# A decode attention block: key loads in runs of 16 KB, on half of the partitions each

## The chip, the core and the metric

The kernel runs on one core of a Trainium2 chip. Its time is the device time of one execution in microseconds (us). The core has five engines that run beside each other: TensorE (PE in the profile; PEld is its weight loads), VectorE (DVE), ScalarE (ACT), GpSimd (POOL) and SyncE (SP), which here issues the large transfers. Transfers from HBM into SBUF are moved by 16 DMA engines. SBUF and PSUM have 128 partitions.

## What is computed

Eight sequences (B = 8) take one decode step. The input is normalized; one branch is attention with 32 query heads and 8 key/value heads over the last W = 1024 of 4096 cached keys, the other a gated FFN whose result gates the attention's.

```python
W = min(4096, max(256, Sk // 4))                       # 1024
xn = _layernorm(x, axis=-1)
q = (xn @ wq) in 32 heads of 128
k, v = the last W rows of k_cache, v_cache, each of 8 heads used by 4 query heads
p = _softmax(q . k * Dh ** -0.5)
s = (p . v) @ wo
g = _silu((_gelu(xn @ w_gate) * (xn @ w_up)) @ w_down)
return x + s * g
```

All inputs are bf16. Keys and values of the window are 2 MB each for a head over all eight sequences (16.8 MB of keys, 16.8 MB of values); wq and wo are 4.2 MB each, the three FFN weights 1.8 MB each. That is 47.45 MB that go through the core once.

## The kernel before

**Tiling.** A *set* is four of the eight sequences for one key/value head (G = 4). There are NS = 16 sets, two for each head (NB = 2; set y of a head holds the sequences 2g + y). The keys of a set lie over 128 partitions: partition 4p + g holds 32 successive keys (8 KB) of sequence g, p = 0 to 31 (KP = 32, NCH = 32). Keys are taken as pairs, and a pair's 256 bf16 values are seen as 128 fp32 values, so that one fp32 transpose on TensorE turns 128 pairs at once.

**Loads.** `load_pair` (L104 to L116) brings both sets of a head into one tile of the pool `big` (nine buffers of 16 KB per partition) with one transfer of 2 MB (L109), or in two of 1 MB, one for each set and each over all partitions (L115; the first head of keys and the last of values). The runs in HBM are 8 KB. wq, the FFN weights, keys, values and wo all use tiles of this pool in turn; wo comes in five pieces (L623 to L627, issued at L130). All are issued by SP, in program order, each waiting until the buffer that it overwrites has been used and until the eighth transfer before it has landed (eight completion semaphores are used in turn). `fetch` (L554) issues them in the order K0, K1, K2, w_down, V0, K3, V1, K4, ... V4, K7, V5, V6, V7.

**Order of the work.** The order on each engine is the program's order, written out by hand in one loop (L571 to L604) over steps t. For a set s the steps are:

- `transpose_quarter(s, 0..3)` (L430) at t = 2s and 2s + 1: four fp32 transposes each into one PSUM tile, copied to `kT` in SBUF by DVE (L444) and ACT (L446) in turn. `kT` holds one set.
- `scores(s)` (L450) at t = 2s + 2, `maxima(s)` (L471) at 2s + 3, `exponentials(s)` (L485) and `turn(s)` (L496, a 32x32 block transpose of the probabilities) at 2s + 4.
- `value_half(s, 0..1)` (L504) at t = 2s + 9 and 2s + 10 (LV = 9), and `gather(h)` (L520), which sums a head's parts and divides by the sum of the exponentials, at t = 4h + 13.
- The FFN's second matmul (`down`, L398) and its gate at t = 8 to 10.

After the loop `project` (L609) multiplies by wo, DVE gates and adds x (L633, L634), and two small transfers write the output.

The score of a key must stand where the value of the same key stands: `own`, `turn` and `value_half` all take keys in the order (p, g) in which the values lie on the partitions.

Of the kernel before, what the change touches and what calls it, by code (L numbers as in the profile page):

```python
# [11 lines left out]
BF16 = mybir.dt.bfloat16  # L12
FP32 = mybir.dt.float32
# [4 lines left out]
def kernel(  # L18
# [13 lines left out]
    nc = tc.nc  # L32

    B, Sq, D = A_x.shape
    Hkv, Sk, Dh = A_k_cache.shape[1], A_k_cache.shape[2], A_k_cache.shape[3]
    Hq = A_wq.shape[1] // Dh
    rep = Hq // Hkv
    W = min(4096, max(256, Sk // 4))
    win0 = Sk - W
# [4 lines left out]
    P = nc.NUM_PARTITIONS  # L44
# [3 lines left out]

    G = 4
    NB = B // G
    NS = Hkv * NB
    KP = P // G
    NCH = W // KP
    NC = G * rep
    SET = NCH * Dh
    QT = 4
    CP = NCH // 2
    QP = CP // QT  # L60
# [7 lines left out]


    lead = ctx.enter_context(tc.tile_pool(name="lead", bufs=1))  # L70
    big = ctx.enter_context(tc.tile_pool(name="big", bufs=9))
    kT_pool = ctx.enter_context(tc.tile_pool(name="kT_pool", bufs=2))
    p_pool = ctx.enter_context(tc.tile_pool(name="p_pool", bufs=2))
    consts = ctx.enter_context(tc.tile_pool(name="consts", bufs=1))
# [3 lines left out]
    ps_kT = ctx.enter_context(tc.tile_pool(name="ps_kT", bufs=4, space=PSUM))  # L78
# [15 lines left out]
    def load_rows(w, r0, n, per, name):  # L94

        t = big.tile([P, 2 * SET], BF16, name="big")
        cols = w.shape[1]
        nc.sync.dma_start(  # L98
            out=t[:, 0 : n * cols],
            in_=w.rearrange("(p k) n -> p k n", p=P)[:, r0 : r0 + n, :],  # L100
        )
        return t[:, 0 : n * cols].rearrange("p (k n) -> p k n", k=n)

    def load_pair(cache, h, parts=1):  # L104

        t = big.tile([P, NB, SET], BF16, name="big")
        src = cache[:, h, win0:Sk, :]
        if parts == 1:
            nc.sync.dma_start(  # L109
                out=t, in_=src.rearrange("b (p c) d -> p b (c d)", p=KP)  # L110
            )
        else:
            src = src.rearrange("(g y) (p c) d -> y p g (c d)", y=NB, p=KP)
            for y in range(NB):
                nc.sync.dma_start(out=t[:, y, :], in_=src[y])  # L115
        return [t[:, y, :].rearrange("p (c d) -> p c d", c=NCH) for y in range(NB)]  # L116

    HB = 2 * SET // (rep * D)
    wo_tiles = {}
# [23 lines left out]
    for k0, cuts in ((0, (1, 1)), (2, (2,))):  # L143
        t = big.tile([P, 2, Hq * Dh], BF16, name="big")
        i = 0
        for n in cuts:
            nc.sync.dma_start(  # L147
                out=t[:, i : i + n, :],
                in_=A_wq.rearrange("(p k) n -> p k n", p=P)[:, k0 + i : k0 + i + n, :],
# [277 lines left out]

    K, V, kT, sc, P_, pT, blk = {}, {}, {}, {}, {}, {}, {}

    def transpose_quarter(s, i):  # L430
        ps = ps_kT.tile([P, QP, P], FP32, name="kT_ps")
        for c in range(QP):
            nc.tensor.transpose(  # L433
                ps[:, c, :],
                K[s][:, 2 * (i * QP + c) : 2 * (i * QP + c) + 2, :]
                .rearrange("p c d -> p (c d)").bitcast(FP32),
                identf,
            )
        if i == 0:
            kT[s] = kT_pool.tile([P, CP, P, 2], BF16, name="kT")  # L440
        out = kT[s][:, i * QP : (i + 1) * QP].rearrange("p c k e -> p (c k e)")
        in_ = ps.rearrange("p c k -> p (c k)").bitcast(BF16)
        if i % 2 == 0:
            nc.vector.tensor_copy(out=out, in_=in_)  # L444
        else:
            nc.scalar.activation(out=out, in_=in_, func=ACT.Copy)  # L446
# [2 lines left out]

    def scores(s):  # L450
        ps = ps_sc.tile([P, CP, 32], FP32, name="sc")
        t = kT.pop(s)
        for e in range(2):
            for R in range(NR):
                nc.tensor.matmul(  # L455
                    ps[32 * R : 32 * R + 32],
                    qT[:, e, s].rearrange("p c b j -> p (c b j)"),
                    t[:, :, 32 * R : 32 * R + 32, e],
                    start=(e == 0), stop=(e == 1), skip_group_check=True,
                )  # L460
        sc[s] = small.tile([P, CP * 32], FP32, name="sc_sb", bufs=2)
        top[s] = small.tile([P, 1], FP32, name="top")
        nc.vector.tensor_tensor_reduce(  # L463
            out=sc[s], in0=ps.rearrange("p c k -> p (c k)"),
            in1=own.rearrange("p c b g -> p (c b g)"),
            op0=ALU.add, op1=ALU.max, scale=1.0, scalar=NEG, accum_out=top[s],
        )
# [3 lines left out]
    def maxima(s):  # L471

        ps = m_top
        nc.tensor.matmul(  # L474
            ps, top.pop(s).to_broadcast([P, P]), identf, start=True, stop=True
        )
        scr = small.tile([P, P], FP32, name="scr", bufs=1)
        bias = small.tile([P, 1], FP32, name="bias")
        nc.vector.tensor_tensor_reduce(  # L479
            out=scr, in0=ps, in1=same.rearrange("p x n -> p (x n)"),  # L480
            op0=ALU.add, op1=ALU.min, scale=-scale, scalar=-NEG, accum_out=bias,
        )
        biases[s] = bias

    def exponentials(s):  # L485
        blk[s] = small.tile([P, 2, Dh + 1], FP32, name="blk", bufs=6)
        P_[s] = p_pool.tile([P, CP * 32], BF16, name="p")
        nc.scalar.activation(  # L488
            out=P_[s], in_=sc.pop(s), func=ACT.Exp, scale=scale, bias=biases.pop(s),
            accum_out=blk[s][:, 0, Dh : Dh + 1],  # L490
        )
        nc.gpsimd.tensor_copy(  # L492
            out=blk[s][:, 1, Dh : Dh + 1], in_=blk[s][:, 0, Dh : Dh + 1]
        )

    def turn(s):  # L496
        pT[s] = p_pool.tile([P, CP, 32], BF16, name="pT", bufs=5)
        nc.vector.transpose(  # L498
            out=pT[s].rearrange("p c k -> p (c k)"), in_=P_.pop(s)
        )  # L500
# [19 lines left out]
    def gather(h):  # L520

        ps = m_out
        for b in range(NB):
            t = blk.pop(h * NB + b)
            for c in range(2):
                nc.tensor.matmul(  # L526
                    ps, sums[:, c, b].rearrange("p j b f -> p (j b f)"), t[:, c, :],
                    start=(b == 0 and c == 0), stop=(b == NB - 1 and c == 1),
                )
        rec = small.tile([P, 1], FP32, name="rec")  # L530
        nc.vector.reciprocal(out=rec, in_=ps[:, Dh : Dh + 1])
        o = small.tile([P, rep, Dh // rep], BF16, name="o")
        nc.vector.tensor_scalar(
            out=o, in0=ps[:, 0:Dh].rearrange("p (i r) -> p r i", r=rep),
            scalar1=rec, scalar2=None, op0=ALU.mult,
        )


        out = oL[:, NS2 * h : NS2 * h + PB, 0:OL]
        out = out.rearrange("p f (r y) -> p r y f", y=OW)  # L540
        nc.vector.transpose(  # L541
            out=out[:, :, 0 : B * NS2 : NS2, :], in_=o.rearrange("p r i -> p (r i)")
        )
# [10 lines left out]
    def fetch(kind, h):  # L554
        while True:
            k, i = pending.pop(0)
            if k == "D":
                down_tiles.append(load_rows(B_w_down, 0, NFC, NFC, "wd"))
            else:
                sets = load_pair(  # L560
                    A_k_cache if k == "K" else A_v_cache, i,
                    2 if (k, i) in (("K", 0), ("V", Hkv - 1)) else 1,
                )
                for y in range(NB):
                    (K if k == "K" else V)[NB * i + y] = sets[y]
            if (k, i) == (kind, h):
                return


    LV = 4 * AHEAD - 3  # L570
    for t in range(2 * NS + LV + 3):  # L571
        s, i = divmod(t, 2)
        if i == 0 and 0 <= s - 2 < NS:
            exponentials(s - 2)
        if s < NS:
            if i == 0 and s % NB == 0:
                fetch("K", s // NB)
            transpose_quarter(s, 2 * i)
        if i == 1 and s >= 6 and s % 2 == 0:
            gather((s - 6) // 2)  # L580
        if s < NS:
            transpose_quarter(s, 2 * i + 1)
        for _ in range(2):
            if hidden_steps:
                hidden_steps.pop(0)()
        if i == 0 and 0 <= s - 2 < NS:
            turn(s - 2)
        if i == 0 and 0 <= s - 1 < NS:
            scores(s - 1)
        if i == 1 and 0 <= s - 1 < NS:  # L590
            maxima(s - 1)
        if t == LV - 1:
            fetch("D", 0)
            down(0)
        if t == LV:
            down(1)
        if t == LV + 1:
            fold()
            gate()
        s3, i3 = divmod(t - LV, 2)  # L600
        if 0 <= s3 < NS:
            if i3 == 0 and s3 % NB == 0:
                fetch("V", s3 // NB)
            value_half(s3, i3)  # L604
# [15 lines left out]
                    skip_group_check=True,  # L620
                )

    pieces = [(0, 0, rep, 4), (4, 0, rep, 2), (6, 0, rep, 1)]  # L623

    pieces += [(Hkv - 1, 0, rep - 1, 1), (Hkv - 1, rep - 1, 1, 1)]
    for h0, r0, nr, nh in pieces:
# [43 lines left out]
```

## Time and profile before

| | |
|---|---|
| Runs | 120.46, 120.54, 120.80 us (median 120.54) |
| Profiled execution | 120.65 us, span 118.8 us from the first to the last instruction |
| Granted TensorE clock | 0.979 on average |
| Bytes read from HBM | 47.46 MB, 400 GB/s over the span |
| Key loads | 7 of 2048 KB, 2 of 1024 KB; median 34.1 and 21.3 us from issue to landing |
| Transposes of keys (L433) | 256, 38.5 us of PE |
| Copies to `kT` | DVE (L444) 32 x 688 ns, ACT (L446) 32 x 1021 ns |

The profile's page gives the busy time of each engine, then the span in 40 equal slices (busy tenths of each engine and of the DMA engines, with GB/s), the DMA queues, the chain of work that ended last, followed back from the last instruction, and the costliest groups of instructions. "SPq" in the chain is SP issuing a transfer. The trace also has a record of each packet that a DMA engine moves, with its size and duration: a packet is one run of bytes into one partition.

### The profile page before, as it was taken

Reading aid. Unit: us, or ns where it says so; the run is one execution under the profiler, and the core shown is the slowest. Engines: PE = TensorE matmul, PEld = TensorE weight load, DVE = VectorE, ACT = ScalarE, POOL = GpSimd, SP = SyncE. Lnnn points to the kernel's source line nnn. Section 1 sums busy time; section 2 is a strip of 40 time slices with the busy share of each in tenths; the row PEclk is TensorE's granted clock in tenths of the full one; section 3 lists DMA queues with packets and bytes.
Section 4 is the critical chain, followed back from the end, with each engine's and each line's share of the span. In section 5 each row is a group of like instructions: output and inputs, shape, how many; then the busy total and the mean of one; then the engine's idle time right before and its main releaser. Section 6 shows DMA issues by size and latency. Waiting matters only on the chain.

```text
span 118.8 us, 2387 instructions
## 1 busy us (share of the span) xinstructions
PE 84.4 (71%) x974; PEld 59.2 (50%) x974; DVE 66.3 (56%) x171; ACT 56.2 (47%) x94; POOL 7.5 (6%) x28
## 2 busy tenths in 40 slices
PE   0070629599492999699969869787795988676670
PEld 0020216198262677377746557555573755555660
DVE  1310131837799766678848658585773965834301
ACT  0500030229808667575854884676565577132000
POOL 7700000000000000000000000000000000000000
PEclk9999999999999599999999999999999999999997
DMA  3999999999999999999999999999999999999940
GB/s 94 430 450 436 406 444 405 433 430 419 422 462 412 412 428 433 417 428 428 425 425 428 422 436 422 422 433 425 425 425 425 428 428 430 408 421 421 420 170 3
DMA packets 6569, 47.60 MB, mean 401 GB/s; under 512 B 536, under 2 KB 672, under 8 KB 1696
## 3 DMA queue, kind: packets, MB, share of 16 engines
q1 hardware_dynamic: 6512, 47.45, 95.2%
q8 instruction: 7, 0.11, 0.3%
q10 hardware_dynamic: 48, 0.01, 0.1%
q14 instruction: 2, 0.02, 0.0%
HBM read 47.46 MB, written 0.01 MB: 400 GB/s over the span
## 4 chain that ended last, share of the span: by engine, by line
DMA 86%; SPq 6%; PE 4%; issue 0%; DVE 0%
DMA big<-in_A_k_cache_dram 72%; DMA big<-in_A_wo_dram 14%; SPq L130 4%; PE kT_ps L433 3%; SPq L147 1%; SPq L98 1%; PE s L615 1%; PE sc L455 0%; DVE tmp L633 0%; DVE out_sb L634 0%; PE o_ps L509 0%
## 5 line engine op out<-in xcount | busy, mean ns | idle before, releaser
L446 ACT ACTIVATE kT<-kT_ps 128x1024 bf16<-128x1024 bf16 x32 | 32.5, 1021 | 23.6 <-PE kT_ps L433 23.5
L433 PE MATMUL kT_ps<-identf,big 128*128 128x128 f32 x256 | 38.5, 296 | 5.2 <-DMA big<-in_A_k_cache_dram 5.1
L433 PEld LDWEIGHTS kT_ps<-identf,big 128*128 128x128 f32 x256 | 30.9, 151 | 13.2 <-DMA big<-in_A_k_cache_dram 7.0
L444 DVE COPY kT<-kT_ps 128x1024 bf16<-128x1024 bf16 x32 | 22.0, 688 | 15.2 <-PE kT_ps L433 15.0
L488 ACT ACTIVATE p<-sc_sb,bias 128x512 bf16<-128x512 f32 x16 | 11.5, 717 | 7.0 <-DVE bias L479 6.5
L509 PE MATMUL o_ps<-big,pT 128*32 128x256 bf16 x256 | 12.3, 274 | 3.0 <-ACT blk L516 1.6
L498 DVE STREAM_TRANSPOSE pT<-p 128x512 bf16<-128x512 bf16 x16 | 11.3, 704 | 2.8 <-ACT p L488 2.8
L474 PE MATMUL m_ps<-identf,top 128*128 128x128 f32 x32 | 7.3, 309 | 6.0 <-DVE top L463 4.3
L463 DVE CUSTOM_DVE_ANT_0 sc_sb<-sc,own 128x512 f32<-128x512 f32 x16 | 10.5, 656 | 0.5 <-PE sc L455 0.5
L455 PE MATMUL sc<-kT,zeros 128*32 128x512 bf16 x128 | 10.3, 398 | 0.5 <-ACT kT L446 0.5
L509 PEld LDWEIGHTS <-pT 128*32 128x32 bf16 x256 | 5.8, 94 | 8.0 <-DMA big<-in_A_v_cache_dram 2.2
L526 PE MATMUL m_ps<-blk,sums 128*128 128x129 f32 x64 | 9.3, 286 | 0.0
L492 POOL COPY blk<-blk 128x1 f32<-128x1 f32 x16 | 2.9, 184 | 96.5 <-ACT p L488 92.2
L474 PEld LDWEIGHTS m_ps<-identf,top 128*128 128x128 f32 x32 | 4.8, 187 | 8.1 <-DVE top L463 5.0
L526 PEld LDWEIGHTS m_ps<-blk,sums 128*128 128x128 f32 x64 | 8.1, 191 | 0.9 <-issue 0.2
L516 ACT ACTIVATE blk<-o_ps 128x256 f32<-128x256 f32 x16 | 6.1, 381 | 3.0 <-PE o_ps L509 3.0
L541 DVE STREAM_TRANSPOSE oL<-o 128x128 bf16<-128x128 bf16 x8 | 6.0, 748 | 0.3
L310 PE MATMUL sc<-big,zeros 128*32 128x512 bf16 x16 | 2.5, 611 | 4.6 <-DMA big<-in_A_wq_dram 4.2
L615 PE MATMUL s<-big,oL 128*32 128x128 bf16 x128 | 4.3, 219 | 1.9 <-DMA big<-in_A_wo_dram 1.9
L317 DVE CAST q_row<-sc 128x512 bf16<-128x512 f32 x2 | 1.3, 686 | 7.8 <-PE sc L310 7.8
L615 PEld LDWEIGHTS <-oL 128*32 128x32 bf16 x128 | 3.8, 96 | 2.5 <-issue 2.3
L479 DVE CUSTOM_DVE_ANT_0 scr<-m_ps,same 128x128 f32<-128x128 f32 x16 | 4.9, 304 | 0.1
(70 smaller groups left out, 51.5 us busy)
## 6 DMA issues: line engine op xcount, KB each, us to landing
big<-in_A_k_cache_dram SPq DMA_DIRECT2D x7, 2048.0 KB, 34.1
big<-in_A_v_cache_dram SPq DMA_DIRECT2D x7, 2048.0 KB, 33.1
big<-in_A_wq_dram SPq DMA_DIRECT2D x2, 1024.0 KB, 5.8
big<-in_A_wq_dram SPq DMA_DIRECT2D x1, 2048.0 KB, 11.2
big<-in_A_k_cache_dram SPq DMA_DIRECT2D x2, 1024.0 KB, 21.3
big<-in_A_v_cache_dram SPq DMA_DIRECT2D x2, 1024.0 KB, 30.3
big<-in_A_wo_dram SPq DMA_DIRECT2D x1, 2048.0 KB, 30.9
big<-in_B_w_gate_dram SPq DMA_DIRECT2D x1, 1792.0 KB, 15.0
```

What stands on the lines that cost most here:

```text
L433: nc.tensor.transpose(ps[:, c, :], K[s][:, 2 * (i * QP + c) : 2 * (i * QP + c) + 2, :] .rearrange("p c d -> p (c d)").bitcast(FP32), identf,)
L444: nc.vector.tensor_copy(out=out, in_=in_)
L446: nc.scalar.activation(out=out, in_=in_, func=ACT.Copy)
L455: nc.tensor.matmul(ps[32 * R : 32 * R + 32], qT[:, e, s].rearrange("p c b j -> p (c b j)"), t[:, :, 32 * R : 32 * R + 32, e], start=(e == ...
L463: nc.vector.tensor_tensor_reduce(out=sc[s], in0=ps.rearrange("p c k -> p (c k)"), in1=own.rearrange("p c b g -> p (c b g)"), op0=ALU.add, ...
L474: nc.tensor.matmul(ps, top.pop(s).to_broadcast([P, P]), identf, start=True, stop=True)
L488: nc.scalar.activation(out=P_[s], in_=sc.pop(s), func=ACT.Exp, scale=scale, bias=biases.pop(s), accum_out=blk[s][:, 0, Dh : Dh + 1],)
L498: nc.vector.transpose(out=pT[s].rearrange("p c k -> p (c k)"), in_=P_.pop(s))
L509: nc.tensor.matmul(o_ps[s][32 * q : 32 * q + 32].rearrange("p c d -> p (c d)"), pT[s][:, c, :], V[s][:, 2 * c : 2 * c + 2, :].rearrange("p ...
L516: nc.scalar.activation(out=blk[s][:, :, 0:Dh], in_=o_ps.pop(s), func=ACT.Copy)
L526: nc.tensor.matmul(ps, sums[:, c, b].rearrange("p j b f -> p (j b f)"), t[:, c, :], start=(b == 0 and c == 0), stop=(b == NB - 1 and c == 1),)
L615: nc.tensor.matmul(s_ps[32 * g : 32 * g + 32, :], t[:, a : a + OW], w[:, q * 128 : (q + 1) * 128], start=(h == 0 and r == 0 and s == 0), s ...
```

## The change

- Keys get a loader of their own, `load_keys`. For each set y of a head one transfer brings its keys to 64 partitions (64y to 64y + 63): partition 64y + 4p + g holds 64 successive keys (16 KB) of sequence 2g + y, p = 0 to 15. A head takes two transfers of 1 MB, all heads 16. Values are loaded as before.
- One transpose now turns 64 pairs of each of the two sets. `transpose_part(h, i)`, i = 0 to 7, replaces the quarters of two sets; each has four transposes and one copy, so that the counts stay the same. A partition of keys holds the keys of two partitions of values (u = 0, 1), so each transpose writes its columns into PSUM with a gap: runs of four (g), then four left out for the other u, at places (y, c, p, u, g). With that the order (p, u, g) is that of the values. `kT` now holds a head (two buffers as before, each twice as large).
- To make room the pool `big` has eight buffers instead of nine.
- `scores`, `maxima`, `exponentials` and `turn` of set s are two steps later (t = 2s + 4, 2s + 5, 2s + 6, 2s + 6). `value_half`, `gather` and the FFN stay at their steps.
- wo is loaded in six pieces: its first four heads come in two transfers instead of one.

```diff
-    big = ctx.enter_context(tc.tile_pool(name="big", bufs=9))
+    big = ctx.enter_context(tc.tile_pool(name="big", bufs=8))
...
+    def load_keys(h):
+        t = big.tile([P, NB * SET], BF16, name="big")
+        src = A_k_cache[:, h, win0:Sk, :].rearrange(
+            "(g y) (p c) d -> y p g (c d)", y=NB, p=KP // NB
+        )
+        for y in range(NB):
+            nc.sync.dma_start(out=t[y * P // NB : (y + 1) * P // NB, :], in_=src[y])
+        return t.rearrange("p (c d) -> p c d", d=Dh)
...
-    def transpose_quarter(s, i):
-        ps = ps_kT.tile([P, QP, P], FP32, name="kT_ps")
-        for c in range(QP):
-            nc.tensor.transpose(
-                ps[:, c, :],
-                K[s][:, 2 * (i * QP + c) : 2 * (i * QP + c) + 2, :]
-                .rearrange("p c d -> p (c d)").bitcast(FP32),
-                identf,
-            )
+    def transpose_part(h, i):
+        ps = ps_kT.tile([P, NB, QP // NB, KP // NB, NB, G], FP32, name="kT_ps")
+        for c in range(QP // NB):
+            for u in range(NB):
+                k0 = u * NCH + 2 * (i * QP // NB + c)
+                nc.tensor.transpose(
+                    ps[:, :, c, :, u, :],
+                    K[h][:, k0 : k0 + 2, :].rearrange("p c d -> p (c d)").bitcast(FP32),
+                    identf.rearrange("p (y b g) -> p y b g", y=NB, g=G),
+                )
         if i == 0:
-            kT[s] = kT_pool.tile([P, CP, P, 2], BF16, name="kT")
+            kT[h] = kT_pool.tile([P, NB, CP, P, 2], BF16, name="kT")
...
     def scores(s):
-        t = kT.pop(s)
+        t = kT[s // NB][:, s % NB]
...
     for t in range(2 * NS + LV + 3):
-        s, i = divmod(t, 2)
-        if i == 0 and 0 <= s - 2 < NS:
-            exponentials(s - 2)
+        h, i = divmod(t, 4)
+        s = due(t, 6)
+        if s is not None:
+            exponentials(s)
...
-    pieces = [(0, 0, rep, 4), (4, 0, rep, 2), (6, 0, rep, 1)]
+    pieces = [(h, 0, rep, 2) for h in range(0, Hkv - 2, 2)] + [(Hkv - 2, 0, rep, 1)]
```

(`due(t, d)` gives s where t = 2s + d.)

More of the change, by code (lines that the diff above doesn't have):

```diff
@@ L428 @@
     K, V, kT, sc, P_, pT, blk = {}, {}, {}, {}, {}, {}, {}
-    def transpose_quarter(s, i):
-        ps = ps_kT.tile([P, QP, P], FP32, name="kT_ps")
-        for c in range(QP):
-            nc.tensor.transpose(
-                ps[:, c, :],
-                K[s][:, 2 * (i * QP + c) : 2 * (i * QP + c) + 2, :]
-                .rearrange("p c d -> p (c d)").bitcast(FP32),
-                identf,
-            )
+    def transpose_part(h, i):
[8 more added lines that the diff above has]
+                )
         if i == 0:
-            kT[s] = kT_pool.tile([P, CP, P, 2], BF16, name="kT")
-        out = kT[s][:, i * QP : (i + 1) * QP].rearrange("p c k e -> p (c k e)")
-        in_ = ps.rearrange("p c k -> p (c k)").bitcast(BF16)
+            kT[h] = kT_pool.tile([P, NB, CP, P, 2], BF16, name="kT")
+        n = QP // NB
+        out = kT[h][:, :, i * n : (i + 1) * n].rearrange("p y c k e -> p y (c k e)")
+        in_ = ps.rearrange("p y c b u g -> p y (c b u g)").bitcast(BF16)
         if i % 2 == 0:
@@ L558, in fetch @@
                 down_tiles.append(load_rows(B_w_down, 0, NFC, NFC, "wd"))
-            else:
[L560 to L563, printed above, removed]
+            elif k == "K":
+                K[i] = load_keys(i)
+            else:
+                sets = load_pair(A_v_cache, i, 2 if i == Hkv - 1 else 1)
                 for y in range(NB):
-                    (K if k == "K" else V)[NB * i + y] = sets[y]
+                    V[NB * i + y] = sets[y]
             if (k, i) == (kind, h):
@@ L570, with due @@
     LV = 4 * AHEAD - 3
+    def due(t, d):
+        s, r = divmod(t - d, 2)
+        return s if r == 0 and 0 <= s < NS else None
     for t in range(2 * NS + LV + 3):
-        s, i = divmod(t, 2)
-        if i == 0 and 0 <= s - 2 < NS:
-            exponentials(s - 2)
[L575 to L582, printed above, removed]
+        h, i = divmod(t, 4)
+        s = due(t, 6)
+        if s is not None:
+            exponentials(s)
+        if h < Hkv:
+            if i == 0:
+                fetch("K", h)
+            transpose_part(h, 2 * i)
+        if i == 1 and h >= 3:
+            gather(h - 3)
+        if h < Hkv:
+            transpose_part(h, 2 * i + 1)
         for _ in range(2):
@@ L585 @@
                 hidden_steps.pop(0)()
[L586 to L591, printed above, removed]
+        if s is not None:
+            turn(s)
+        s = due(t, 4)
+        if s is not None:
+            scores(s)
+        s = due(t, 5)
+        if s is not None:
+            maxima(s)
         if t == LV - 1:
```

## The prediction

> **What bounds the kernel now.** I read the head of the page first (span and engine shares), then the row of DMA shares, then the chain of work that ended last.
>
> ```profile
> span 118.8 us, 2387 instructions
> PE 84.4 (71%) x974; PEld 59.2 (50%) x974; DVE 66.3 (56%) x171; ACT 56.2 (47%) x94; POOL 7.5 (6%) x28
> ...
> DMA  3999999999999999999999999999999999999940
> ...
> q1 hardware_dynamic: 6512, 47.45, 95.2%
> ...
> DMA 86%; SPq 6%; PE 4%; issue 0%; DVE 0%
> ```
>
> No compute engine is over 71%, while the DMA engines are full in 37 of 40 slices, 95.2% of the span on the one queue, and the chain is 86% DMA. So this is a stream of 47.45 MB, and the end is the stream's end plus a short tail. The tail is read in the chain in order of time:
>
> ```profile
> 97.86 17.15 DMA big<-in_A_wo_dram
> 115.00 0.04 issue
> 115.05 0.64 PE s L615 x16
> 115.68 0.02 issue
> 115.71 0.29 DVE tmp L633
> 116.00 0.02 issue
> 116.03 0.28 DVE out_sb L634
> ```
>
> The last piece of wo lands at 115.0; 3.8 us of matmul, two DVE steps and the output transfer follow. What lengthens or shortens the stream by x us moves the end by x us, as long as the stream never runs dry and compute keeps up. Next I asked what the stream's rate depends on, with a table by stretches (the columns after the stretch: its length, busy time of PE, PEld, DVE, ACT, POOL, granted clock, DMA share, GB/s):
>
> ```profile
> 7.00:12.00 5.00, 1.71 (x16) 0.44 (x9) 0.00 (x0) 0.00 (x0) 0.00 (x0) 1.00 1.03 442
> 12.00:20.50 8.50, 5.44 (x52) 2.76 (x51) 1.76 (x4) 1.29 (x3) 0.00 (x0) 1.00 1.01 430
> ...
> 45.00:99.00 54.00, 45.93 (x526) 32.92 (x524) 37.72 (x97) 34.89 (x59) 2.02 (x11) 1.00 1.01 427
> 104.50:112.00 7.50, 5.82 (x123) 4.91 (x124) 3.22 (x7) 1.37 (x4) 0.18 (x1) 1.00 1.02 421
> ```
>
> By the order of issue these are mostly 16 KB packets (the third wq load), 14 KB packets (gate and up), 8 KB packets (keys and values) and 4 KB packets (wo). The rate is 442, 430, 427, 421 GB/s: almost a cap on bytes, with a little lost per packet. The trace's records of single packets say it more exactly (medians): 159 ns for 4 KB, 309 for 8 KB, 611 for 16 KB. So a packet costs about 7 ns and then 27.1 bytes per ns, on each of 16 engines.
>
> **The change, part by part.** The sum is made against the profiled execution: 120.65 us, of which 118.8 are span and 1.85 lie around it; the median of the three runs is 120.54, 0.1 lower.
>
> *Longer runs.* Keys are 8 heads x 2 MB = 16.8 MB: before, 2048 packets of 8 KB, 128 per engine, 128 x 309 ns = 39.55 us. After, 1024 packets of 16 KB, 64 per engine, 64 x 611 = 39.10 us. Gain 0.45 us, all on the bounding stream.
>
> *More transfers.* Keys go in 16 transfers instead of 9, wo in 6 instead of 5. Each ends with a completion write of 9 ns per engine (the 4-byte packets of the trace): 8 x 9 ns = 0.07 us, on the stream. That two transfers of 1 MB instead of one of 2 MB cost nothing else is seen in the first head, which already goes in two (L115, each over all partitions), with the shares around it full. The issue time on SP (0.6 us where it does not wait) is hidden: SP issues some 30 us ahead of landing.
>
> *SP's order and its waits.* SP issues each transfer only after the eighth transfer before it has landed (eight completion semaphores in turn). Before, eight transfers ahead were up to 16 MB; now a head of keys takes two of the eight, so that eight hold some 8 x 1.4 = 11 MB, 26 us of stream. One buffer fewer (8 instead of 9) means that each load waits for a consumer one load earlier. The tightest that I find is the value load of head 4, which waits for the values of head 0, used just after the keys of head 3 land; six loads (V1, K4, V2, K5, V3, K6, about 12 MB) may stand behind those keys. So the stream stays fed: cost nothing, cover over 20 us; if it broke, each us of starvation would be a us at the end.
>
> *The partitions.* This is the disputed part. Each transfer of keys now writes 64 partitions instead of 128, with all 16 engines still on it. No row of before shows a large transfer on fewer than 128 partitions, so I bound it. Lower end: nothing, if the cap of 27.1 bytes per ns belongs to the engines; a gain beyond the 0.45 us is excluded, since the engines are already full and only the 7 ns per packet can be saved. Upper end: if the cap belongs to where the bytes enter SBUF (427 GB/s over 128 partitions, 3.3 GB/s for each), 64 partitions take 213 GB/s, a 16 KB packet lasts 1222 ns and keys last 78.2 us: +39.1 us. The two halves of a head do not make this good by overlapping: each engine takes its transfers in order, all 16 have equal work in each, and so all are in the lower half together and then all in the upper half. The rows near it: the two halves of the first head at full rate, but each over all partitions; and x_sb, eight packets of 1 KB on eight partitions, 44 ns each where the 1 KB packets of wo on 128 partitions take 46, which speaks for the lower end but is too short to fill anything. Against it: the cap hardly moves with packet length or source tensor, so it is neither HBM nor the handling of packets; what is left is the engine and its entry to SBUF, and a DMA share of 1.0 fits both, because an engine held up by its destination counts as busy. I take the upper end, as a choice and not a reading: all the cap's rows are taken with every partition in use, and the change halves just that.
>
> [...]
>
> *Transposes.* Count unchanged: 256 of 128x128 fp32. Eight in a row take 1.09 us (136 ns each). New is that each result is written to PSUM in runs of four fp32 with gaps of four. Nothing in the trace is written so. Between nothing and double (256 x 136 ns = 35 us more PE, on 84.4 of 118.8), I take nothing: a column of 128 results every 1.06 ns leaves its writing the same number of elements, in runs of 16 bytes. The evacuations (DVE 688 ns, ACT 1021 ns) keep their element counts, in two runs of 512 instead of one of 1024: nothing. Transposes now wait for both halves of a head; for the first head that is 2.4 us later (23.86 to about 26), hidden because PE next waits for w_down, which lands behind all of the first three heads of keys anyway.
>
> *Scores, maxima, exponentials* come two steps of the loop later, values stay where they were (exponentials of a set three steps ahead of its values): nothing, since in before the transposed last output (L541) is done at 110.8 and the last wo lands at 115.0. wo's first piece in halves lets its first matmuls start earlier, which the last piece hides.
>
> Sum: 120.65 - 0.45 + 0.07 + 39.1 = 159.4; against the median 0.1 lower, I say 159.
>
> **Rivals.** (1) *The engines hold the cap* and halves run at full rate: 120.65 - 0.38 = 120.3, not slower than before. It decides at one point: a 16 KB packet of keys takes 611 ns, not 1222. For it: the x_sb packets; the engines' full share. Against it: only that the case is untried in these rows. (2) *Partial sharing*: two engines meet at the same entry only while they are level; one that is ahead by d of the 2.44 us of a half (4 x 611 ns) saves 2d per head. If they settle out of step after a head or two, the cost is 5 to 10 us (125 to 131); with a steady lead of 0.5 us it is 39.1 - 8 x 1.0 = 31 (151). (3) *The gapped PSUM writes double the transposes*, the halves at full rate: PE 84.4 + 35 = 119 us busy, more than the span, in a kernel that also waits for the first keys until 24 us: 24 + 74.5 (PE busy from there on, by the stretches) + 35 = about 134. (4) *A dry stream*, from eight transfers in flight with a buffer less: gaps in the DMA row at each head; 1 us per head would give 128. The waits above speak against it.
>
> **Numbers.** Half rate throughout 0.52 (159), partial sharing 0.13 (125 to 151), engines hold the cap 0.28 (120.3), gapped writes or a dry stream 0.07 (122 to 134). A measurement of this kernel tells about 0.3% (0.36 us) from no change. Rival 1 lies at -0.32%, right at that bound: of its 0.28 I put 0.14 on faster, 0.13 on the same, 0.01 on slower. Faster 0.14, same 0.13, slower 0.73. The range goes from just under rival 1 (the median basis and a few tenths) to just over half rate: 119.7 to 162. The likeliest case alone: 150 to 162.
>
> **What would show it.** Right: mean GB/s near 210 in the stretches of keys and 427 in those of values, with the DMA share still near 1; time to landing of keys longer; PE, DVE and ACT busy times unchanged and their idle time "<-DMA ... k_cache"; span near 157. Wrong: GB/s at 430 in all slices (rival 1); alternation that fades after the first heads (rival 2); transposes of 270 ns each in a run (rival 3); zeros in the DMA row (rival 4).

## The result, and the profile after

The changed kernel takes 166.8 to 177.6 us in six runs (median 169.6) against 120.46 to 120.80 in six runs of the kernel before (median 120.59). Over the comparable runs the ratio is 1.39, 95% interval 1.3865 to 1.3935; runs over 1.5% above the fastest of the same kernel are left out of it, which is why it is a little below the ratio of the medians. The profiled execution took 168.24 us, 47.6 more than before.

The head of the page after the change, then the DMA rows of the 40 slices, the queue and the shares of the chain:

```profile
span 166.4 us, 2388 instructions
PE 96.5 (58%) x974; PEld 68.4 (41%) x974; DVE 67.5 (41%) x171; ACT 56.9 (34%) x94; POOL 7.6 (5%) x28
...
DMA  5999999999999999899999999999999999999910
GB/s 197 435 430 431 427 228 232 205 228 213 224 202 399 417 287 224 232 415 207 209 319 335 217 207 287 313 219 205 305 295 215 203 315 423 429 419 415 404 70 2
...
q1 hardware_dynamic: 5616, 47.45, 94.9%
...
DMA 81%; PE 12%; DVE 2%; ACT 1%; issue 1%; SPq 0%; ACTq 0%
```

The DMA engines are as full as before (the row of nines, 94.9%) and move the same 47.45 MB, but the rate falls from some 425 GB/s to 202 to 232 wherever only keys are loaded, and comes back in between. The table by stretches shows it without the slices' mixing: inside the first three heads of keys, w_down and the first values after them, and the end of the values (the last three columns are granted clock, DMA share and GB/s):

```profile
24.00:45.00 21.00, 9.13 (x48) 8.08 (x48) 7.76 (x11) 6.74 (x8) 0.00 (x0) 0.58 1.01 218
51.00:56.00 5.00, 2.04 (x23) 1.18 (x23) 2.14 (x6) 2.12 (x4) 0.18 (x1) 1.00 0.99 420
...
138.00:150.00 12.00, 10.62 (x115) 7.38 (x113) 8.81 (x23) 6.67 (x11) 0.37 (x2) 0.92 1.01 426
```

The engines count as busy (a DMA share of 1.01) and move half as much (218 GB/s): here each packet took longer. The trace's packet records agree: the 1024 packets of keys take 1203 ns on average, where 16 KB took 611 before.

The 47.6 us divide as follows (packet records, summed and divided by 16 engines):

| | us |
|---|---|
| Keys: 64 packets per engine x (1203 - 611 ns) | +37.9 |
| Longer runs and more completions (-0.45 + 0.07, as worked out ahead) | -0.4 |
| Values: 2048 packets at 363 ns on average, 310 before | +6.8 |
| w_down: 128 packets at 598 ns on average, 535 before | +0.5 |
| Rest of the stream (what is left of the 46.0; the engines end further apart, below) | +1.2 |
| Together: landing of the last wo piece (115.0 before, 161.0 after) | +46.0 |
| From that landing to the end of the last wo matmul (0.7 before, 2.3 after) | +1.6 |

The 16 engines do not end together. In the last two us before the last landing, their DMA share was 0.59 before (first line) and is 0.17 now (second line):

```profile
113.00:115.00 2.00, 1.51 (x48) 1.24 (x43) 0.00 (x0) 0.00 (x0) 0.00 (x0) 1.00 0.59 222
159.00:161.00 2.00, 2.00 (x57) 1.88 (x58) 1.25 (x3) 0.00 (x0) 0.00 (x0) 1.00 0.17 64
```

The end shows the last row of the table. In the chain in order of time there is no transfer any more after the last keys, which land at 137.0 us:

```profile
158.44 1.20 PE m_ps L543 x8
159.64 3.70 PE s L640 x128
163.34 0.02 issue
163.37 0.29 DVE tmp L658
```

All 128 wo matmuls run in one piece behind the last gather; before, the last 16 of them waited for the last piece of wo.

### The profile page after: what moved, and what is told of

The parts are those of the page before. It is cut to its first block, busy times and chain, and to the rows that moved or that the text cites. A ratio compares the mean times of both kernels' runs of the same rounds, so it can differ in the third digit from the quotient of the medians.

```text
span 166.4 us, 2388 instructions
## 1 busy us (share of the span) xinstructions
PE 96.5 (58%) x974; PEld 68.4 (41%) x974; DVE 67.5 (41%) x171; ACT 56.9 (34%) x94; POOL 7.6 (5%) x28
## 3 DMA queue, kind: packets, MB, share of 16 engines
q1 hardware_dynamic: 5616, 47.45, 94.9%
## 4 chain that ended last, share of the span: by engine, by line
DMA 81%; PE 12%; DVE 2%; ACT 1%; issue 1%; SPq 0%; ACTq 0%
DMA big<-in_A_k_cache_dram 49%; DMA big<-in_A_v_cache_dram 25%; DMA big<-in_A_wq_dram 7%; PE m_ps L543 3%; PE kT_ps L450 3%; PE s L640 2%; PE o_ps L526 2%; PE sc L472 1%; ACT kT L463 1%; PE m_ps L491 1%; ACT p L505 0%; SPq L160 0%; DVE oL L558 0%; DVE o L550 0%; DVE pT L515 0%
## 5 line engine op out<-in xcount | busy, mean ns | idle before, releaser
L450 PE MATMUL kT_ps<-identf,big 128*128 128x128 f32 x256 | 45.9, 336 | 39.4 <-DMA big<-in_A_k_cache_dram 39.4
L450 PEld LDWEIGHTS kT_ps<-identf,big 128*128 128x128 f32 x256 | 37.1, 174 | 47.7 <-issue 32.3
L526 PE MATMUL o_ps<-big,pT 128*32 128x256 bf16 x256 | 14.2, 308 | 6.3 <-DMA big<-in_A_v_cache_dram 5.8
L472 PE MATMUL sc<-kT,zeros 128*32 128x512 bf16 x128 | 12.9, 487 | 0.5 <-ACT kT L463 0.5
L526 PEld LDWEIGHTS <-pT 128*32 128x32 bf16 x256 | 6.4, 106 | 13.3 <-issue 7.4
L543 PE MATMUL m_ps<-blk,sums 128*128 128x129 f32 x64 | 11.3, 332 | 0.0
L543 PEld LDWEIGHTS m_ps<-blk,sums 128*128 128x128 f32 x64 | 10.4, 242 | 0.9 <-issue 0.8
L472 PEld LDWEIGHTS <-zeros 128*32 128x32 bf16 x128 | 2.2, 100 | 4.2 <-issue 2.2
L323 PEld LDWEIGHTS <-zeros 128*32 128x32 bf16 x32 | 1.1, 120 | 6.9 <-issue 6.3
```

Source lines behind the costliest of these rows:

```text
L450: nc.tensor.transpose(ps[:, :, c, :, u, :], K[h][:, k0 : k0 + 2, :].rearrange("p c d -> p (c d)").bitcast(FP32), identf.rearrange("p (y b ...
L472: nc.tensor.matmul(ps[32 * R : 32 * R + 32], qT[:, e, s].rearrange("p c b j -> p (c b j)"), t[:, :, 32 * R : 32 * R + 32, e], start=(e == ...
L526: nc.tensor.matmul(o_ps[s][32 * q : 32 * q + 32].rearrange("p c d -> p (c d)"), pT[s][:, c, :], V[s][:, 2 * c : 2 * c + 2, :].rearrange("p ...
L543: nc.tensor.matmul(ps, sums[:, c, b].rearrange("p j b f -> p (j b f)"), t[:, c, :], start=(b == 0 and c == 0), stop=(b == NB - 1 and c == 1),)
```

## The experiments

One theory and three rivals stood at the start. *Entry*, the choice of the prediction: 64 partitions take half of the 427 GB/s that 128 take, so each transfer of keys runs at half the rate. *Rivals*: the 16 KB runs are read slowly from HBM (A); something in the rest of the change costs (B); more and smaller transfers (C). Where no ratio is given, a kernel was timed once; times of one kernel scatter by up to 23 us where the keys load at half rate, and such a kernel lies 40 us and more above one at full rate.

**One whole transfer, still 16 KB runs**

```diff
-        src = A_k_cache[:, h, win0:Sk, :].rearrange(
-            "(g y) (p c) d -> y p g (c d)", y=NB, p=KP // NB
-        )
-        for y in range(NB):
-            nc.sync.dma_start(out=t[y * P // NB : (y + 1) * P // NB, :], in_=src[y])
+        src = A_k_cache[:, h, win0:Sk, :]
+        nc.sync.dma_start(
+            out=t, in_=src.rearrange("b (p c) d -> p b (c d)", p=KP // NB)
+        )
...
```

> Edit: the changed kernel, but each head of keys in one transfer of 2 MB over all 128 partitions, still in runs of 16 KB (partition 8p + 2g + y); the transposes write their columns at the places that bring the same final order, now single fp32 values with gaps. Everything else (eight buffers, later scores, wo in six pieces) as in the changed kernel. Theory (the entry into SBUF: a transfer to half of the partitions gets half the rate): key packets back to 611 ns, stream at 425 to 440 GB/s, 120.2 us, 0.3% under before. Rival A (runs of 16 KB or their addresses in HBM are read slowly): packets stay near 1250 ns, about 166. Rival B (something in the rest of the change: buffers, steps of the loop, gapped writes): well over 121 with packets at 611 ns.

Ratio 1.391 (1.3832 to 1.3983), 166.7 to 189.6 us: as slow as the change, with all 128 partitions in each transfer. Its DMA rows, from an execution of 176.0 us:

```profile
DMA  6999999999999998999899999999999999999100
GB/s 192 442 433 428 407 214 222 211 218 218 211 281 411 378 229 190 393 260 218 214 393 205 199 258 320 207 214 286 277 214 179 299 376 416 420 421 368 71 32 2
```

In the first three heads of keys it is the same 211 to 222 GB/s. So "half of the partitions" can't be the whole cause, and my theory in that form fell.

**The halves alone**

```diff
-        if parts == 1:
+        if parts == 1 and cache is A_k_cache:
+            src = src.rearrange("b (p c) d -> p b (c d)", p=KP)
+            for z in (0, 1):
+                nc.sync.dma_start(
+                    out=t[z * P // 2 : (z + 1) * P // 2],
+                    in_=src[z * KP // 2 : (z + 1) * KP // 2],
+                )
+        elif parts == 1:
```

> Edit: the kernel before, with one thing changed: heads 1 to 7 of the keys come in two transfers of 1 MB, partitions 0 to 63 and 64 to 127, runs of 8 KB, same layout, same nine buffers, same transposes. Theory (entry): key packets of 8 KB go from 309 to 620 to 640 ns; 7 of 8 heads pay what the change paid on 8 (45.5 us of stream), so +35 to +40 us: 156 to 161. Rival A (16 KB runs): 120.6. Rival B (rest of the change): 120.6.

161.6 us, in one run: just above the range expected. Rivals A and B are out as the main cause: runs of 8 KB, nine buffers, old layout, and still +41 us. (A half of 32 steps has 16 steps in its source, as in the changed kernel, so this run does not part the two faults that are told apart below.)

**Two transfers per head, each over all partitions**

```diff
-                    2 if (k, i) in (("K", 0), ("V", Hkv - 1)) else 1,
+                    2 if k == "K" or (k, i) == ("V", Hkv - 1) else 1,
```

> Edit: the kernel before, with every head of keys in two transfers of 1 MB, one per set, each over all 128 partitions (as the first head is already). Same number of transfers on the queue as in the changed kernel. Theory (entry): 120.6, no difference beyond 0.1 us. Rival C (more transfers, eight completion semaphores that now hold 11 MB instead of 16 in flight): slower, in the case of the whole loss 160 or more.

Ratio 1.0011 (1.0001 to 1.002). Rival C is out: the number of transfers and the bytes in flight cost 0.1 us.

**Quarters**

```diff
...
+            for z in (0, 1, 2, 3):
+                nc.sync.dma_start(
+                    out=t[z * P // 4 : (z + 1) * P // 4],
+                    in_=src[z * KP // 4 : (z + 1) * KP // 4],
+                )
...
```

> Edit: as the kernel before with heads 1 to 7 of the keys in four transfers of 512 KB on 32 partitions each, runs of 8 KB, same layout. It parts two forms of the theory. Each partition has its own share of the rate (as my prediction put it, 3.3 GB/s each): 32 partitions take 107 GB/s, packets about 1240 ns, keys of seven heads 138 us instead of 34.6, some 224 us. Groups of partitions share an entry and 0 to 31 reach as many as 0 to 63: packets 620 to 640 ns as with halves, 156 to 161 us, and fewer bytes in flight (the eight transfers hold some 7 MB) still hidden. Rivals A and B: 120.6.

177.3 us, between the two expectations, and the profile says why neither fits. Three stretches in the keys:

```profile
58.00:61.00 3.00, 1.43 (x15) 0.31 (x12) 0.29 (x2) 1.29 (x3) 0.18 (x1) 0.50 0.51 216
61.00:64.00 3.00, 3.00 (x20) 1.71 (x16) 1.31 (x2) 0.88 (x1) 0.00 (x0) 0.50 0.51 216
64.00:67.00 3.00, 2.27 (x20) 1.87 (x21) 1.20 (x4) 1.29 (x4) 0.00 (x0) 0.50 0.51 216
```

The DMA share is 0.51: only half of the engines work, each at its full speed (the 8 KB packets in these stretches have a median of 309 ns). The source of a quarter has 8 outer steps (p), and by the share eight engines of 16 got work. I read from it that the outer dimension of the source decides how a transfer is dealt to engines. It is not so all the time: from 32 to 38 and from 125 to 134 us the share is 1.05 and 1.03, 8 KB packets take some 640 ns and the rate is 216 and 212 GB/s. And 32 partitions take 216 GB/s, 6.75 GB/s each, twice what my prediction gave a partition at most: the limit is not one of single partitions.

That gave a new theory, an estimate of mine from these numbers that no trace shows: the slow packets take about twice the time of the fast ones (some 640 for 309 ns here, 1203 for 611 in the changed kernel), as if two engines met at one entry, and which engines meet follows from the dealing of a transfer, set by its outer dimensions, and from the partitions that it writes. Four runs vary the steps of the source (16 or 32) and the partitions (lower and upper half, all, even and odd), at 16 KB runs; the changed kernel is 16 steps, lower and upper half.

**32 steps, lower and upper half**

```diff
-        src = A_k_cache[:, h, win0:Sk, :].rearrange(
-            "(g y) (p c) d -> y p g (c d)", y=NB, p=KP // NB
+        src = A_k_cache[:, h, Sk - 2 * W : Sk, :].rearrange(
+            "(y g) (p c) d -> y p g (c d)", g=NB, p=KP
         )
```

> After the run with one whole transfer (16 KB runs to all 128 partitions, as slow as the changed kernel) the theory that half of the partitions is the cause, by itself, has fallen. What the slow transfers have in common is that their source's outermost dimension has 16 steps (p = 0 to 15), one for each engine; the fast ones have 32 or 128. New theory: the outermost dimension decides which rows go to which engine; with 16, engines meet two by two at one entry into SBUF. This edit: the changed kernel, each transfer of keys still 64 partitions and 16 KB runs, but source dimensions 32 x 2 instead of 16 x 4 (2048 rows of two sequences instead of 1024 of four: other keys are read, the same bytes; the output is not the reference's). If partitions matter as well (64 of them have half of the entries, whatever the dealing): packets near 1250 ns and 160 to 175 us. If the outer dimension alone matters: packets 611 ns, 120.2 us.

171.2 us: halves are slow with 32 steps too.

```profile
24.00:45.00 21.00, 8.38 (x44) 7.76 (x48) 7.89 (x12) 6.31 (x8) 0.00 (x0) 0.58 1.01 215
```

**32 steps, all partitions** (the edit against the first experiment)

```diff
-        src = A_k_cache[:, h, win0:Sk, :]
-        nc.sync.dma_start(
-            out=t, in_=src.rearrange("b (p c) d -> p b (c d)", p=KP // NB)
-        )
+        src = A_k_cache[:, h, Sk - 2 * W : Sk, :].rearrange(
+            "(g y) (p c) d -> y p g (c d)", y=NB, p=KP
+        )
+        nc.sync.dma_start(out=t, in_=src[0])
```

> Edit: the run with one whole transfer, source dimensions 32 x 4 instead of 16 x 8 (2048 rows of four sequences; other keys are read, the same bytes; the output is not the reference's). Still 16 KB runs, 128 partitions, one transfer of 2 MB. Theory (outer dimension decides the dealing): packets 611 ns, stream at 430 GB/s, 120.2 us. Rival (16 KB runs at distances of megabytes are read slowly from HBM, whatever the dealing): packets stay near 1250 ns, 166 us or more.

Ratio 0.9983 (0.9966 to 1.0), ten runs from 120.2 to 123.2 us, median 120.8. The difference to the first experiment is the source's dimensions alone (and with them which keys are read, the same bytes), and 46 us are gone; rival A is out. One stretch of keys in the first experiment, one here, and the DMA row here:

```profile
24.00:30.00 6.00, 0.00 (x0) 0.00 (x0) 0.13 (x1) 0.00 (x0) 0.00 (x0) 0.58 1.01 218
...
21.00:36.00 15.00, 9.76 (x72) 7.33 (x72) 8.66 (x22) 7.64 (x11) 0.00 (x0) 0.89 1.00 428
...
GB/s 99 421 451 440 419 428 445 429 418 418 429 434 453 399 470 423 388 423 432 440 410 459 434 399 445 429 404 429 448 421 415 423 434 423 407 426 421 408 76 3
```

The last piece of wo lands 0.3 us earlier than before (114.7), which is what the longer runs promised, but in the profiled execution (121.08 us) the time does not follow: the wo matmuls start only at 112.4, behind the last gather, and end at 116.1 (before: 115.7).

**Halves from a contiguous source**

```diff
-        src = A_k_cache[:, h, win0:Sk, :].rearrange(
-            "(g y) (p c) d -> y p g (c d)", y=NB, p=KP // NB
-        )
+        src = A_k_cache[0:NB, h, :, :].rearrange("y (p c) d -> y p (c d)", p=P // NB)
```

> Edit: the changed kernel, each transfer of keys 64 partitions and 16 KB runs, but from one stretch of 1 MB that is contiguous in HBM (64 rows of 16 KB, all 4096 keys of one sequence; other keys are read, the same bytes; the output is not the reference's). Nothing in the read is strided and the outer dimension has 64 steps. If the half of the partitions costs by itself: packets near 1250 ns, 160 to 175 us, as in the changed kernel. If only the outer dimension of 16 or the strides of the read cost: 120.2 us.

173.6 us, 212 GB/s from 24 to 45 us. Nothing of the read is strided, so the half itself costs, on the writing side.

**32 steps, even and odd partitions** (the edit against the run with 32 steps and halves)

```diff
-            nc.sync.dma_start(out=t[y * P // NB : (y + 1) * P // NB, :], in_=src[y])
+            nc.sync.dma_start(out=t[y:P:NB, :], in_=src[y])
```

> Edit: the run with halves and source dimensions 32 x 2 (64 partitions, 16 KB runs, slow), with one thing changed: the first transfer of a head writes the even partitions, the second the odd ones, instead of the lower and the upper half (other keys are read, the same bytes; the output is not the reference's). If 64 partitions have half the rate because there are 64 of them, whichever they are: packets near 1250 ns, 160 to 175 us. [...]

120.9 us, where a rate that depends on which partitions are written was put at 120 to 121. As many partitions per transfer, 64, the same bytes, the same reads as with 32 steps and halves; only which partitions are written differs:

```profile
24.00:45.00 21.00, 15.40 (x107) 12.60 (x107) 12.95 (x26) 11.79 (x16) 0.25 (x2) 0.92 1.00 424
45.00:99.00 54.00, 46.38 (x541) 33.39 (x535) 38.51 (x99) 35.65 (x59) 2.16 (x12) 1.00 1.01 427
```

424 GB/s where halves had 215. This run shows one half of the cause: not how many partitions a transfer writes, but which.

**16 steps, even and odd partitions**, the edit above in the changed kernel, with the transposes' output order to fit.

> Edit: the changed kernel with the right keys (source dimensions 16 x 4, 16 KB runs, two transfers of 64 partitions per head), but the first transfer of a head writes the even partitions and the second the odd ones; the transposes' output order is changed to fit. With 32 source steps this was as fast as before (120.9 us). [...]

166.6 us, 228 GB/s from 24 to 45 us; key packets 1139 ns on average. Put ahead were 160 to 180 us by the dealing theory, and 121 to 122.3 if even partitions are enough. Even partitions do not help when the source has 16 steps, as the dealing theory has it. How the 16 steps go to the engines was not shown: the trace does not tell which engine a packet is on.

**Only the later steps**

```diff
-    big = ctx.enter_context(tc.tile_pool(name="big", bufs=9))
-    kT_pool = ctx.enter_context(tc.tile_pool(name="kT_pool", bufs=2))
+    big = ctx.enter_context(tc.tile_pool(name="big", bufs=8))
+    kT_pool = ctx.enter_context(tc.tile_pool(name="kT_pool", bufs=3))
...
-        if i == 0 and 0 <= s - 2 < NS:
-            exponentials(s - 2)
+        if i == 0 and 0 <= s - 3 < NS:
+            exponentials(s - 3)
...
-            turn(s - 2)
+            turn(s - 3)
-            scores(s - 1)
+            scores(s - 2)
-            maxima(s - 1)
+            maxima(s - 2)
```

> Edit: the kernel before with its loads as they were, and of the change only the later steps: scores, maxima, exponentials and turn two steps later (a third kT buffer for that) and eight instead of nine buffers in the pool big. My prediction put this at nothing. The run with 32 x 4 source dimensions made me doubt it: its stream ends earlier, but its 128 wo matmuls start only at 112.3 us after the last gather and run 3.7 us back to back. If the later steps push the last gather past its slack: wo matmuls end near 116.1 instead of 115.7, +0.4 us, 121.0. If not: 120.6 within 0.1.

Ratio 1.0131 (1.0114 to 1.0148), 122.3 us: +1.6 us, more than either number. The last wo piece lands at 115.06, as before, so the eight buffers cost nothing; the end is compute:

```profile
110.48 1.04 PE o_ps L509 x13
111.53 2.02 PE m_ps L526 x8
113.55 3.89 PE s L615 x65
117.46 0.29 DVE tmp L633
```

The last gather's eight matmuls took 2.02 us here; in before they were done by 109.4 and took 1.27. The granted clock from 104.5 to 112 was 0.67, against 1.00 before. Other kernels with later steps have such a stretch near the end too: the clock is 0.50 from 107.1 to 113.9 us here, from 107.8 to 111.2 with 32 steps and all partitions, and from 153.6 to 157.0 in the changed kernel. So a lower clock is part of the cost; how much of it was not separated. This run sets a size for the later steps in the old order of transposes; in the changed order at full rate (32 steps, all partitions) the wo matmuls end only 0.4 us later than before, so the cost hangs on what stands around the steps.

**The second halves from another queue**

```diff
-            nc.sync.dma_start(out=t[y * P // NB : (y + 1) * P // NB, :], in_=src[y])
+            (second if y and second else nc.sync).dma_start(
+                out=t[y * P // NB : (y + 1) * P // NB, :], in_=src[y]
+            )
...
+        if t % 4 == 3 and h + AHEAD < Hkv:
+            fetch("K", h + AHEAD)
```

> Edit: the changed kernel, with the second half of heads 3 to 7 issued from ScalarE's queue, three heads ahead of its use, the first half from SP's as before. Each engine then has two lists, and takes packets of an upper half between packets of whole transfers or lower halves. If the loss comes from all engines being in the same half at the same time (my prediction's reason), mixing recovers part of it: under 155 us, down to about 140 (five heads of eight full). If two engines meet at an entry whatever the order: 165 to 175 us, as before.

171.6 us: nothing recovered. The keys on ScalarE's queue (five transfers of 1 MB) landed a median 15.1 us after their issue, those on SP's 41.6, which fits a mixing of the two queues' packets. Key packets fell to 1145 ns on average (1203 in the changed kernel, 3.7 us over all keys), but those of values rose to 383 (363) and those of w_down to 780 (598), which is 3.9 us. My reading is that mixing moves the meeting of two engines to other transfers and does not remove it.

## Why the prediction was right and wrong

- **The bound**: right. The stream's last landing moved by 46.0 of the 47.6 us, and transfers are 81% of the chain.
- **Direction and the size of the main term**: right. Half rate, keys +37.9 us where I had 39.1. The reason given for it was only half right (below), so that the size was partly luck: each of two faults gives half the rate (halves with 32 steps 215 GB/s, all partitions with 16 steps 218), and both together no less (218).
- **The total**: wrong. 159 was forecast, at most 162; 166.8 to 177.6 came. The profiled execution is 8.8 us over the sum of 159.4, by terms and rounded: keys -1.2, values +6.8, w_down +0.5, the rest of the stream +1.2, the end +1.6. The terms that failed are three that I put at nothing.
  - First, the values: +6.8 us. I had said that all 16 engines are in the lower half together and then in the upper half. They do not stay level, and rival 2, which allowed for that, counted a lead as a gain alone; here keys gained 1.2 us and values lost 6.8. The packet records show where: the 1449 packets of values that have no packet of keys in flight beside them take 313 ns on average, the other 599 take 484, and these hold 6.5 of the 6.8 us. In the run with 32 steps and all partitions, values take 310 ns on average, beside keys or not. My reading is that an engine already in the values shares an entry with one still in the keys; which pairs meet is argued, since the trace does not name the engine of a packet. That the engines end apart is in the share of 0.17 above; in the profiled run with one whole transfer it is 0.13 from 163 to 167 us, about two engines of 16. Such meetings would also explain part of why these kernels scatter by some 6 to 14% and the kernel before by 0.3%; not all of it, since the run with 32 steps and all partitions scatters by 2.5%.
  - Second, the scores' later steps (0.4 to 1.6 us in the runs that show them, 1.6 at the end of the changed kernel), where I counted L541 as done at 110.8 and forgot that all the wo matmuls, 3.7 us in one piece, stand behind the last gather in PE's order. In before they started at 110.4 and ended at 115.7, so that the slack was some 1.6 us and not the 4.2 from 110.8 to 115.0.
  - Third, w_down, 0.5 us: the 33 of its packets with keys in flight beside them take 759 ns on average, the others 542.
- **"3.3 GB/s for each partition"**: wrong as a mechanism. Quarters took 6.75 GB/s per partition, even partitions the full rate with 64, and one transfer over all 128 partitions half the rate. The kernel before could have told: a packet goes into one partition, and 8 KB in 309 ns are 26.5 GB/s. What the runs show is that two things decide the rate: which partitions a transfer writes, and the outer steps of its source. With 32 steps, halves took 215 GB/s and even and odd partitions 424; over all partitions, 16 steps took 218 and 32 steps 428. Why is not shown: that the dealing and the partitions set how many engines meet at an entry is my estimate, which fits them all. The change had both faults: halves, and a source of 16 steps. Mending one alone left it slow (32 steps and halves 171.2; 16 steps and all partitions 166.7 and more).
- **Nothing for more transfers, eight in flight, one buffer fewer**: right (+0.1 us for the transfers; no gap in the DMA row of after).
- **Nothing for the gapped PSUM writes**: right. With gaps, eight transposes take 1.04 us in the critical chain of the changed kernel where the clock is full, and the median transpose is 273 ns in both kernels; PE is busy 84.0 us in the run with 32 steps and all partitions, 84.4 before.
- **Rival 1** (engines hold the cap) and the rest: out, by the runs above. Of the x_sb packets that spoke for it, seven took 44 ns and one 475. Its 120.3 is what 16 KB runs bring at best with a good dealing: three of the ten runs with 32 steps and all partitions took 120.2 to 120.4 us.

## What to carry to other kernels

Before reshaping a load for longer runs, look at its source's outer dimension and at the partitions that it writes, and time both: over all partitions 32 outer steps ran at 428 GB/s here (128, those of wq, at 442 from 7 to 12 us of the kernel before) and 16 at 218, and 8 steps on 32 partitions at 216; with 32 steps, even and odd partitions ran at 424, the lower and the upper half at 215. A DMA row full of nines with half the GB/s was here a matter of how the loads were shaped: the share was 1.01 at 215 GB/s and 1.00 at 424, with the same reads. And a step moved later in a hand-written order can be paid at the end of the kernel, where nothing follows to hide it (0.4 to 1.6 us here).

## What the runs showed of the hardware that was not expected

- A transfer over all 128 partitions ran at 218 GB/s (24 to 30 us of the run with one whole transfer) with a source of 16 outer steps, and at 428 with 32 (21 to 36 us).
- Eight engines alone (a DMA share of 0.51) reached 216 GB/s on 32 partitions, where sixteen (1.01) on 64, lower and upper half, reached 212 to 218.
- A packet of values takes 484 ns on average with packets of slowly written keys in flight beside it, and 313 without; beside keys at full rate it takes 310.
- TensorE's granted clock fell to 0.50 in stretches after it had waited for keys. One such pair of stretches of the changed kernel stands first below: TensorE is busy for 0.03 of 3.5 us, and then has a clock of 0.50. From 24 to 45 us the clock was 0.58 on average, and the mean key transpose rose from 296 to 336 ns (the last two lines, before and after).

```profile
58.00:61.50 3.50, 0.03 (x4) 0.03 (x7) 0.00 (x0) 0.97 (x3) 0.18 (x1) 1.00 1.18 328
61.50:64.90 3.40, 3.40 (x24) 1.82 (x23) 1.31 (x2) 0.87 (x1) 0.00 (x0) 0.50 0.99 217
...
L433 PE MATMUL kT_ps<-identf,big 128*128 128x128 f32 x256 | 38.5, 296 | 5.2 <-DMA big<-in_A_k_cache_dram 5.1
L450 PE MATMUL kT_ps<-identf,big 128*128 128x128 f32 x256 | 45.9, 336 | 39.4 <-DMA big<-in_A_k_cache_dram 39.4
```
